# Linear attention with a gated channel mix on one core: q (batches 3 to 7) and y (batches 6 and 7) transposed by DMA in place of TensorE

## The chip, the cores and the metric

The kernel runs on one core of one Trainium2 chip. The metric is the device time of one execution in microseconds (us), the median of several runs. Matmuls run on TensorE (PE, its weight loads PEld), elementwise work on VectorE (DVE) and ScalarE (ACT). GpSimd (POOL) asks for the loads, SyncE (SP) for the stores.

## The reference

Eight batches, eight heads, 576 tokens, head size 64; then a channel mix of 512 channels with 1024 hidden ones:

```python
kv = np.einsum('bhsd,bhse->bhde', k, v)
out = np.einsum('bhsd,bhde->bhse', q, kv)
rms = np.sqrt(np.mean(out * out, axis=-1, keepdims=True) + 1e-06)
x = heads_side_by_side(out / rms * g_norm)              # B, S, 512
x_prev = x shifted by one token, zero first
xk = mu_k * x + (1.0 - mu_k) * x_prev
xr = mu_r * x + (1.0 - mu_r) * x_prev
k = np.maximum(xk @ w_k, 0.0)
v = k * k @ w_v
r = 1.0 / (1.0 + np.exp(-(xr @ w_r)))
return r * v
```

## The kernel before, in words

One loop runs over the batches, b = 0 to 7. In each, TensorE goes through three stages of units, and `mix` writes out the order of all engines by hand: after unit i of a stage the steps that `put(stage, i, ...)` listed are issued. K is the first product: eight units (`km`), each with eight matmuls into `ps_km`, a relu on ACT into `rt` and a square into `sqk` on DVE or ACT (`ACT_SQ`). R is the gate (`r`): four or five tiles of 128 tokens into `ps_r`, a sigmoid on ACT. V is the second product (`vv`): two half units a tile into `ps_v`, then a product with the sigmoid on DVE (`finish`) and two stores on SP's queue. Even batches have four tiles, odd ones five, as two batches share nine. An engine takes its instructions in the order in which they were issued.

Between these units stands the attention of later batches. While batch b is mixed, a = b+1 gets its last attention steps and a2 = b+2 its first (in batches 2 to 5 fully so):

- `kv`: 72 matmuls on quadrants of TensorE (64x64), two copies to SBUF.
- `qt`: 72 transposes of q on TensorE (L188) into `ps_qt`, copied to `qT` by ACT (three) and DVE (one) (L113, L115).
- `u`: 40 matmuls qT by kv into `ps_u` (L210); `square` on ACT and `reduce` on DVE give the sums of squares `ss`.
- `newton`: eight small DVE instructions for 1/rms; `mult` writes y = u/rms on DVE (L253).
- `flip`, `flip0`: 36 transposes of y on TensorE (L268) into `ps_x`; `move` (ACT and DVE, L258, L260) scales by g and writes `xT`, channels by tokens.
- `wrap`, `diff`, and `scale` and `add` (together `blend`): the token shift, giving `xk` and `xr` (L343 to L370). The next batch's K needs xk, its R needs xr.

The attention has five PSUM banks in turn (`ps_at`), the mix three (`ps_mm`). The inputs of a batch have one buffer each (`in_k`, `in_v`, `in_q`), so `load_all(b + 3)`, in the order k, v, q on POOL's queue, waits until kv and qt of batch b+2 have read theirs. `out_sb` has seven buffers, `rt` seven, most others two. Batches 0 and 1 have an order of their own.

Of the kernel before, what the change touches and what calls it, by code (L numbers as in the profile page):

```python
# [24 lines left out]
def kernel(  # L25
# [13 lines left out]
    nc = tc.nc  # L39
# [55 lines left out]

    def load_all(b):
        if b < B:
            for name in "kvq":
                x_in[name, b] = inp.tile([128, NHP, GX], BF16, tag=f"in_{name}", name=f"in_{name}")
                nc.gpsimd.dma_start(out=x_in[name, b], in_=by_token(dram[name], b))  # L100

# [120 lines left out]
    def newton(a):  # L222


        ss = at[a]["ss"]
        ms, y, t, s = (mine(a, key, [128, NRG, NHP], FP32) for key in ("ms", "rs", "nt", "ns"))

        def first():
            DVE.tensor_scalar(out=ms, in0=ss, scalar1=1.0 / HD, scalar2=1e-6, op0=ALU.mult, op1=ALU.add)

        def guess():
            DVE.tensor_scalar(out=y.bitcast(I32), in0=ms.bitcast(I32), scalar1=-0.5,
                              scalar2=float(0x5F1FFFF9), op0=ALU.mult, op1=ALU.add)

        def squared():
            DVE.tensor_mul(out=t, in0=y, in1=y)

        def halve(c):
            DVE.scalar_tensor_tensor(out=s, in0=t, scalar=c, in1=ms, op0=ALU.mult, op1=ALU.mult)

        def update(c):
            DVE.scalar_tensor_tensor(out=y, in0=s, scalar=c, in1=y, op0=ALU.add, op1=ALU.mult)

        steps = [first, guess]
        for c in (0.703952253, 0.5):
            steps += [squared, lambda c=c: halve(-c), lambda c=c: update(1.5 if c == 0.5 else c * 2.38924456)]
        return steps

    def mult(a, t0, n, Ms):
        y, rs, cts = mine(a, "y", [128, NRG, NHP, HD], BF16), at[a]["rs"], span(Ms)  # L250
        for i, ps in enumerate(at[a]["u", t0, n, Ms]):
            g = rg(t0, n, i) if n else slice(0, 1)
            DVE.tensor_mul(out=y[:, g, cts], in0=ps,  # L253
                           in1=rs[:, g, cts].unsqueeze(3).to_broadcast([128, max(n, 1), 2 * len(Ms), HD]))

    def move(eng, dst, src):
        if eng is ACT:
# [115 lines left out]
    def km_part(b, fcs, c0, c1, dst, eng=ACT, which=ps_mm):  # L373
        ps = bank(which, [128, len(fcs), c1 - c0], FP32, "ps_km")
        for n, fc in enumerate(fcs):
            for cc in range(NHP):
                nc.tensor.matmul(ps[:, n, :], wk_sb[:, cc, 128 * fc:128 * fc + 128], at[b]["xk"][:, cc, c0:c1],  # L377
                                 start=(cc == 0), stop=(cc == NHP - 1))
# [20 lines left out]

    sig, hold, later = {}, {}, {}  # L400

    def r(t):
        ps = bank(ps_mm, [128, C], FP32, "ps_r")
        for cc in range(NHP):
            nc.tensor.matmul(ps, xr[:, cc, 128 * t:128 * t + 128], wr_sb[:, cc, :],  # L405
                             start=(cc == 0), stop=(cc == NHP - 1))
        sig[t] = work.tile([128, C], BF16, tag="sig", name="sig", bufs=6)
        ACT.activation(out=sig[t], in_=ps, func=AF.Sigmoid)  # L408
# [31 lines left out]
    def mix(b, plan):  # L440
# [15 lines left out]
        units += [("R", i, lambda t=t: r(t)) for i, t in enumerate(tiles)]  # L456
# [75 lines left out]
    rs_c("y1", odd, *lx)  # L532

    every = slice(0, NHP)
    for b in range(B):
        a, a2 = b + 1, b + 2
        plan = {}

        def put(stage, i, *steps):
            plan.setdefault((stage, i), []).extend(steps)  # L540
# [2 lines left out]
            return lambda: f(*args)  # L543

        load_all(b + 3)

        def attend(a, stage, i):

            put(stage, i, on(kv, a, ALL, (ACT, ACT)), on(qt, a, 0, (ACT, DVE)), on(qt, a, 1, (ACT, ACT)))

        def all_u(a, stage, i):
            put(stage, i, on(u, a, 2, 2, ALL), on(u, a, 0, 2, ALL), on(u, a, 0, 0, ALL),
                on(square, a, 2, 2, ALL), on(square, a, 0, 2, ALL), on(square, a, 0, 0, ALL))

        def mults(a):
            return [on(mult, a, 2, 2, ALL), on(mult, a, 0, 2, ALL), on(mult, a, 0, 0, ALL)]

        def flips(a):
            return [on(flip, a, 0, 4, ALL, (ACT, DVE)), on(flip0, a, (ACT, ACT))]

        def blend(a, which, eng=DVE):
# [33 lines left out]
        elif b == 1:  # L595
            br = blend(1, 1)
            put("K", 1, on(kv, a, ALL, (ACT, ACT), (ps_at, ps_at)))
            put("K", 3, on(qt, a, 0, (ACT, DVE)), on(qt, a, 1, (DVE, DVE)))
            put("K", 4, *br[:3])
            put("K", 5, *br[3:])  # L600
            put("K", 6, part_square(1, slice(0, 8), *hi1))
            put("K", 7, on(u, a, 2, 2, ALL), on(u, a, 0, 2, ALL), on(u, a, 0, 0, ALL), on(square, a, 2, 2, ALL),
                on(reduce, a, 5, 9, ALL))
            put("K", 8, on(square, a, 0, 2, ALL), part_square(1, slice(0, 2), *lo1))
            put("K", 9, on(square, a, 0, 0, ALL))
            put("K", 10, part_square(1, slice(2, 4), *lo1), on(reduce, a, 0, 5, ALL))
            put("K", 11, part_square(1, slice(4, 6), *lo1), part_square(1, slice(6, 8), *lo1))
            put("R", 1, lambda a=a: run(newton(a)))
            put("R", 4, mults(a)[0])
            put("V", 0, mults(a)[1], mults(a)[2])  # L610
            put("V", 4, *flips(a))
            put("V", 5, on(wrap, a), on(diff, a, every), on(kv, a2, ALL, (ACT, ACT)))
            put("V", 6, *blend(a, 0), on(qt, a2, 0, (ACT, DVE)), on(qt, a2, 1, (ACT, ACT)))
            all_u(a2, "V", 8)
        elif a < B:
            if b == 2:
                br = blend(2, 1)
                put("K", 0, *br[:3])
                put("K", 1, *br[3:])
                put("K", 2, on(reduce, a, 5, 9, ALL))  # L620
                put("K", 3, on(reduce, a, 0, 5, ALL))
                put("K", 5, lambda a=a: run(newton(a)[:4]))
                put("K", 6, lambda a=a: run(newton(a)[4:]))
                put("K", 7, mults(a)[0])
                put("R", 0, mults(a)[1])
                put("R", 1, mults(a)[2])
                put("V", 0, on(kv, a2, ALL, (ACT, ACT)), on(qt, a2, 0, (ACT, DVE)),
                    on(flip, a, 0, 4, ALL, (ACT, DVE)), on(flip0, a, (DVE, DVE)), on(wrap, a), on(diff, a, every))
                put("V", 1, on(qt, a2, 1, (ACT, ACT)))
                put("V", 2, *blend(a, 0)[:3])  # L630
# [31 lines left out]
_INS = ['q', 'k', 'v', 'g_norm', 'moe_mu_k', 'moe_mu_r', 'moe_w_k', 'moe_w_v', 'moe_w_r']  # L662
# [26 lines left out]
```

## Time and profile before

| | |
|---|---|
| Time, median of 3 runs (lowest to highest) | 207.17 us (206.87 to 207.18) |
| Span of the profiled execution, first to last instruction | 205.0 us |
| Time of the profiled execution around its span | not listed apart; the median is 2.2 us above the span |
| Granted TensorE clock | 1.000 |
| ps_v, ps_km, ps_r on PE | 62.0, 65.1 and 32.1 us busy |
| ps_qt on PE (504 transposes) | 6.3 us busy |
| ps_x on PE (252 transposes) | 5.6 us busy |
| Loads of k, v, q, issue to landing | 7.9, 11.1 and 13.8 us |

A profile is one execution; times are us from the start of the span. L12 is line 12 of the kernel. Busy times count an instruction from start to end, and matmuls overlap, so a sum over a group can exceed the time it holds the engine; the chain of waits gives the time that a group holds alone. "idle <-X" names what ended an engine's idle time. The chain follows back from the last instruction to what released it, or to the instruction before it on the same engine.

### The profile page before, as it was taken

What the parts mean: (1) busy time and instruction counts of PE and PEld (TensorE: products, weight loads), DVE (VectorE), ACT (ScalarE), POOL (GpSimd) and SP (SyncE); (2) the same over time, 40 slices, a digit from 0 to 9 for tenths busy, and PEclk for the clock granted to TensorE, in tenths of its full rate; (3) what the DMA queues carried; (4) which work ended last, traced back from release to release, by engine and by line L of the source; (5) the groups of instructions that cost most, each with busy time, mean ns of one, the idle gap of its engine ahead of it and who ended that gap; (6) DMA issues with size and microseconds to landing.
All of it is one profiled execution on the core that took longest, in us unless ns stands there. A gap on an engine that the chain in (4) does not pass through costs nothing.

```text
span 205.0 us, 6284 instructions
## 1 busy us (share of the span) xinstructions
PE 191.3 (93%) x2654; PEld 115.7 (56%) x2684; DVE 156.6 (76%) x333; ACT 137.7 (67%) x290; POOL 24.9 (12%) x40
## 2 busy tenths in 40 slices
PE   7778989999998899999999999999999999999992
PEld 2335854585444685557554674567554674476451
DVE  2479959989979598889879695999688794984131
ACT  2378784578725789868997389868986489267400
POOL 7940130040004000400021000400000000000000
PEclk9999999999999999999999999999999999999999
DMA  6999999999937990799009960599004600160055
GB/s 219 211 205 207 206 208 199 209 212 179 172 67 125 220 207 0 104 209 240 5 8 170 254 180 0 72 224 258 5 3 107 155 0 3 42 155 9 3 121 135
DMA packets 21360, 27.22 MB, mean 133 GB/s; under 512 B 1740, under 2 KB 16340, under 8 KB 21332
## 3 DMA queue, kind: packets, MB, share of 16 engines
q0 software_dynamic: 14848, 16.19, 48.7%
q1 hardware_dynamic: 6244, 10.36, 18.1%
q8 instruction: 21, 0.34, 0.7%
q10 hardware_dynamic: 240, 0.26, 0.4%
q14 instruction: 7, 0.06, 0.1%
HBM read 33.56 MB, written 9.44 MB: 210 GB/s over the span
## 4 chain that ended last, share of the span: by engine, by line
PE 75%; DVE 10%; ACT 6%; DMA 4%; issue 2%; POOL 1%; DVEq 0%; ACTq 0%; POOLq 0%
PE ps_v L415 27%; PE ps_km L377 26%; PE ps_r L405 12%; DMA rt<-in_v_dram 4%; PE ps_u L210 3%; PE ps_x L268 2%; PE ps_kv L174 2%; PE ps_qt L188 2%; ACT sqk L386 1%; ACT rt L380 1%; DVE ss L220 1%; DVE y L253 1%; DVE m L355 1%; DVE sqk L388 1%; ACT sig L408 1%
## 5 line engine op out<-in xcount | busy, mean ns | idle before, releaser
L380 ACT ACTIVATE rt<-ps_km 128x288 bf16<-128x288 f32 (+3 forms) x120 | 50.9, 429 | 21.6 <-PE ps_km L377 13.8
L377 PE MATMUL ps_km<-xk,wk_sb 128*128 128x288 bf16 (+4 forms) x512 | 65.1, 286 | 0.2
L415 PE MATMUL ps_v<-wv_sb,sqk 128*128 128x512 bf16 x265 | 62.0, 379 | 1.8 <-issue 1.4
L377 PEld LDWEIGHTS <-wk_sb 128*128 128x128 bf16 x512 | 49.3, 98 | 15.4 <-issue 1.0
L415 PEld LDWEIGHTS <-sqk 128*128 128x128 bf16 x280 | 26.1, 98 | 30.0 <-issue 0.2
L432 DVE TENSOR_TENSOR out_sb<-ps_v,sig 128x512 f32<-128x512 f32 (+1 forms) x37 | 24.6, 672 | 15.6 <-PE ps_v L415 14.0
L405 PE MATMUL ps_r<-wr_sb,xr 128*128 128x512 bf16 x132 | 32.1, 379 | 0.6
L408 ACT ACTIVATE sig<-ps_r 128x512 bf16<-128x512 f32 x36 | 21.3, 610 | 2.9 <-PE ps_r L405 2.9
L388 DVE TENSOR_TENSOR sqk<-rt 128x576 bf16<-128x576 bf16 (+4 forms) x39 | 19.0, 506 | 4.7 <-ACT rt L380 4.7
L405 PEld LDWEIGHTS <-xr 128*128 128x128 bf16 x144 | 13.7, 98 | 15.1 <-issue 0.3
L216 ACT ACTIVATE sq<-ps_u 128x512 bf16<-128x512 f32 (+1 forms) x35 | 16.6, 564 | 7.2 <-PE ps_u L210 7.2
L253 DVE TENSOR_TENSOR y<-ps_u,rs 128x512 bf16<-128x512 f32 (+1 forms) x35 | 19.8, 628 | 0.3
L220 DVE TENSOR_REDUCE ss<-sq 128x16 f32<-128x1024 bf16 (+1 forms) x14 | 18.4, 1345 | 1.8 <-ACT sq L216 1.8
L258 ACT ACTIVATE xT<-ps_x,cols 128x128 bf16<-128x128 bf16 (+2 forms) x22 | 12.4, 645 | 8.3 <-PE ps_x L268 8.3
L100 POOL DMA_DIRECT2D in_k<-in_k_dram x7 | 5.2, 746 | 101.5 <-PE ps_kv L174 101.5
L113 ACT COPY qT<-ps_qt 128x576 bf16<-128x576 bf16 x19 | 11.4, 648 | 8.8 <-PE ps_qt L314 6.3
L355 DVE TENSOR_SCALAR m<-dx,cols 128x576 bf16<-128x576 bf16 (+2 forms) x52 | 16.2, 357 | 0.2
L347 DVE TENSOR_TENSOR dx<-xT 128x2304 bf16<-128x2304 bf16 (+4 forms) x11 | 11.3, 1029 | 4.1 <-ACT xT L258 3.8
L386 ACT ACTIVATE sqk<-rt 128x576 bf16<-128x576 bf16 x18 | 12.4, 687 | 0.0
L370 DVE TENSOR_TENSOR xr<-m,xT 128x1152 bf16<-128x1152 bf16 x16 | 11.7, 754 | 0.2
L370 DVE TENSOR_TENSOR xk<-m,xT 128x1152 bf16<-128x1152 bf16 (+2 forms) x16 | 11.2, 704 | 0.5
L353 ACT ACTIVATE m<-dx,cols 128x576 bf16<-128x576 bf16 (+2 forms) x14 | 9.4, 725 | 2.5 <-DVE dx L347 2.5
(64 smaller groups left out, 131.6 us busy)
## 6 DMA issues: line engine op xcount, KB each, us to landing
out_dram<-out_sb SPq DMA_DIRECT2D x69, 128.0 KB, 3.6
in_k<-in_k_dram POOLq DMA_DIRECT2D x7, 576.0 KB, 7.9
in_v<-in_v_dram POOLq DMA_DIRECT2D x7, 576.0 KB, 11.1
in_q<-in_q_dram POOLq DMA_DIRECT2D x7, 576.0 KB, 13.8
wk_sb<-in_moe_w_k_dram POOLq DMA_DIRECT2D x2, 512.0 KB, 9.1
wv_sb<-in_moe_w_v_dram POOLq DMA_DIRECT2D x2, 512.0 KB, 21.5
sqk<-in_k_dram SPq DMA_DIRECT2D x1, 576.0 KB
q<-in_q_dram POOLq DMA_DIRECT2D x2, 288.0 KB, 6.4
```

Of the source, the lines that this page charges most:

```text
L216: ACT.activation(out=sq[:, rg(t0, n, i) if n else slice(0, 1), span(Ms)], in_=ps, func=AF.Square)
L220: DVE.tensor_reduce(out=ss[:, g0:g1, span(Ms)], in_=sq[:, g0:g1, span(Ms)], op=ALU.add, axis=AX.X)
L253: DVE.tensor_mul(out=y[:, g, cts], in0=ps, in1=rs[:, g, cts].unsqueeze(3).to_broadcast([128, max(n, 1), 2 * len(Ms), HD]))
L355: eng.tensor_scalar(out=out_, in0=in_, scalar1=mu, scalar2=None, op0=ALU.mult)
L370: DVE.tensor_add(out=dst, in0=m[:, hs, c0:c1], in1=x[:, hs, c0:c1])
L377: nc.tensor.matmul(ps[:, n, :], wk_sb[:, cc, 128 * fc:128 * fc + 128], at[b]["xk"][:, cc, c0:c1], start=(cc == 0), stop=(cc == NHP - 1))
L380: eng.activation(out=dst, in_=ps, func=AF.Relu)
L388: eng.tensor_mul(out=sqk[:, fcs, o:o + n], in0=src, in1=src)
L405: nc.tensor.matmul(ps, xr[:, cc, 128 * t:128 * t + 128], wr_sb[:, cc, :], start=(cc == 0), stop=(cc == NHP - 1))
L408: ACT.activation(out=sig[t], in_=ps, func=AF.Sigmoid)
L415: nc.tensor.matmul(ps, sqk[:, fc, 128 * t:128 * t + 128], wv_sb[:, fc, :], start=(fc == 0), stop=(fc == NFC - 1))
L432: DVE.tensor_mul(out=o, in0=hold[t], in1=sig[t][:, c])
```

## The change

`qt_d` replaces `qt` for batches 3 to 7: one transposing DMA from SP's queue turns the whole q tile of 128x2304 into 18 blocks of 128x128. In such a block head channels stand on the upper or the lower half of the partitions by the parity of the token group, so `kv_d` writes kv a second time with its halves swapped (four more copies on ACT), and `u_d` and `u0_d` work in 72 matmuls on quadrants. `square_d`, `reduce_d` and `mult_d` are the same steps in the new layout. From batch 4 on, loads are asked for in the order q, k, v.

For batches 6 and 7 `flip_d` turns y by six transposing DMAs a batch straight into `xT`, in place of `flip`, `flip0` and `move`. The scaling by g, which `move` did, goes into copies of two weights, `wkg` and `wrg`, which eight POOL instructions, issued in batch 5, write; K and R of batches 6 and 7 use them. For 3 to 5 `flip_p` is `flip` in the new layout.

The order changes with it. In batches 2 to 4 newton and mult stand at K4 to K7, the flip of y with wrap and diff at V0, the blends at V1 to V3 and the adds for xr at K0 of the next batch; kv stands at V1, the transposing DMA of q at K6 and u at V5. In batches 5 and 6 mult stands at K0 to K2 with flip_d right behind each, newton in the batch before. The cut diff:

```diff
+    wkg = const.tile([128, NHP, F], BF16, name="wkg")
+    wrg = const.tile([128, NHP, C], BF16, name="wrg")
...
-            for name in "kvq":
+            for name in "kvq" if b < 4 else "qkv":
                 x_in[name, b] = inp.tile([128, NHP, GX], BF16, tag=f"in_{name}", name=f"in_{name}")
                 nc.gpsimd.dma_start(out=x_in[name, b], in_=by_token(dram[name], b))
...
+    NJ = G // 2
+    NQ = NHP * S // 128
+
+    def qt_d(a):
+        qT_ = at[a]["qT"] = work.tile([128, NQ, 128], BF16, tag="qT", name="qT")
+        nc.sync.dma_start_transpose(out=qT_, in_=x_in["q", a].rearrange("p m x -> p (m x)"))
+
+    def kv_d(a, engines, shifts):
+
+        dst = at[a]["kv"] = work.tile([128, 2, 2, 2, HD], BF16, tag="kv", name="kv")
+        kb, vb = x_in["k", a], x_in["v", a]
+        ps = [bank(ps_at, [128, 2, HD], FP32, "ps_kv") for _ in range(2)]
+        for M in range(2):
+            for j in range(G):
+                for e in range(2):
+                    for i in range(2):
+                        nc.tensor.matmul(ps[e][half(i), M, :], kb[half(e), 2 * M + i, tok(j)],
+                                         vb[half(e), 2 * M + i, tok(j)], start=(j == 0), stop=(j == G - 1))
+        for e in range(2):
+            evac(engines[e], dst[:, 0, e], ps[e])
+        for e in range(2):
+            for i in range(2):
+                evac(shifts[e], dst[half(1 - i), 1, e], ps[e][half(i)])
+
+    def u_one(a, out_, m, e, j):
+        par = (m + j) % 2
+        nc.tensor.matmul(out_, at[a]["qT"][half(par), (G * m + j) // 2, half(e)],
+                         at[a]["kv"][half(par), int(m % 2 != par), e, m // 2, :], start=True, stop=True)
+
+    def u_d(a, t0):
+
+        ps = at[a]["u", t0] = [bank(ps_at, [128, 2, 2, 2, HD], FP32, "ps_u") for _ in range(2)]
+        for t in range(2):
+            for mh in range(2):
+                for e in range(2):
+                    for mp in range(2):
+                        for r in range(2):
+                            u_one(a, ps[mp][half(r), t, mh, e, :], 2 * mh + mp, e, 2 * (t0 + t) + 1 + r)
+
+    def u0_d(a):
+
+        ps = at[a]["u", None] = [bank(ps_at, [128, 2, 2, HD], FP32, "ps_u")]
+        for mh in range(2):
+            for e in range(2):
+                for mp in range(2):
+                    u_one(a, ps[0][half(mp), mh, e, :], 2 * mh + mp, e, 0)
...
+    def mult_d(a, t0):
+        rs = at[a]["rs"]
+        if "yd" not in at[a]:
+            t_ = work.tile([128, 4 * NRG, HD], BF16, tag="y", name="y")
+            at[a]["yd"] = t_[:, 4:].rearrange("p (t h) d -> p t h d", t=NJ), t_[:, 0:4]
...
+    def flip_p(a, engines):
+        y, y0 = at[a]["yd"]
+        ps = [bank(ps_at, [128, NHP, NJ, P], BF16, "ps_x") for _ in range(2)]
+        for t in range(NJ):
+            for hp in range(NHP):
+                for r in range(2):
+                    nc.tensor.transpose(ps[r][:, hp, t, :], y[half(r), t, 2 * hp:2 * hp + 2].rearrange("p e d -> p (e d)"),
+                                        ident[half(r), half(r)])
+        for r in range(2):
+            move(engines[r], blocks(a)[:, :, 1 + r:8 + r:2, :], ps[r])
...
+    def flip_d(a, t0):
+        y, y0 = at[a]["yd"]
+        if t0 is None:
+            for mp in range(2):
+                nc.sync.dma_start_transpose(out=xT[a % 2][:, mp::2, P:2 * P],
+                                            in_=y0[half(mp)].rearrange("p h d -> p (h d)"))
+        else:
+            for t in range(t0, t0 + 2):
+                c0 = P + P * (2 * t + 1)
+                nc.sync.dma_start_transpose(out=xT[a % 2][:, :, c0:c0 + 2 * P], in_=y[:, t].rearrange("p h d -> p (h d)"))
...
-                nc.tensor.matmul(ps[:, n, :], wk_sb[:, cc, 128 * fc:128 * fc + 128], at[b]["xk"][:, cc, c0:c1],
+                nc.tensor.matmul(ps[:, n, :], (wkg if b >= FROM_Y else wk_sb)[:, cc, 128 * fc:128 * fc + 128], at[b]["xk"][:, cc, c0:c1],
...
-            nc.tensor.matmul(ps, xr[:, cc, 128 * t:128 * t + 128], wr_sb[:, cc, :],
+            nc.tensor.matmul(ps, xr[:, cc, 128 * t:128 * t + 128], (wrg if b >= FROM_Y else wr_sb)[:, cc, :],
...
+    FROM_Q, FROM_Y = 3, 6
...
-
-        def attend(a, stage, i):
-
-            put(stage, i, on(kv, a, ALL, (ACT, ACT)), on(qt, a, 0, (ACT, DVE)), on(qt, a, 1, (ACT, ACT)))
+        if b == FROM_Y - 1:
+            for dst, src in ((wkg, wk_sb), (wrg, wr_sb)):
+                for cc in range(NHP):
+                    POOL.tensor_scalar(out=dst[:, cc], in0=src[:, cc], scalar1=g_sb, scalar2=None, op0=ALU.mult)
...
         def mults(a):
+            if a >= FROM_Q:
+                return [on(mult_d, a, 2), on(mult_d, a, 0), on(mult_d, a, None)]
             return [on(mult, a, 2, 2, ALL), on(mult, a, 0, 2, ALL), on(mult, a, 0, 0, ALL)]
 
+        def turns(a):
+            return [on(flip_d, a, 2), on(flip_d, a, 0), on(flip_d, a, None)]
+
+        def sums(a):
+            if a >= FROM_Q:
+                return [on(reduce_d, a, 20, 36), on(reduce_d, a, 0, 20)]
+            return [on(reduce, a, 5, 9, ALL), on(reduce, a, 0, 5, ALL)]
+
         def flips(a):
+            if a >= FROM_Q:
+                return [on(flip_p, a, (ACT, DVE)), on(flip0_p, a, (ACT, ACT))]
...
-            put("V", 5, on(wrap, a), on(diff, a, every), on(kv, a2, ALL, (ACT, ACT)))
-            put("V", 6, *blend(a, 0), on(qt, a2, 0, (ACT, DVE)), on(qt, a2, 1, (ACT, ACT)))
+            put("V", 0, on(qt_d, a2))
+            put("V", 5, on(wrap, a), on(diff, a, every), on(kv_d, a2, (ACT, ACT), (ACT, ACT)))
+            put("V", 6, *blend(a, 0))
             all_u(a2, "V", 8)
-                put("K", 2, on(reduce, a, 5, 9, ALL))
-                put("K", 3, on(reduce, a, 0, 5, ALL))
-                put("K", 5, lambda a=a: run(newton(a)[:4]))
-                put("K", 6, lambda a=a: run(newton(a)[4:]))
-                put("K", 7, mults(a)[0])
-                put("R", 0, mults(a)[1])
-                put("R", 1, mults(a)[2])
-                put("V", 0, on(kv, a2, ALL, (ACT, ACT)), on(qt, a2, 0, (ACT, DVE)),
-                    on(flip, a, 0, 4, ALL, (ACT, DVE)), on(flip0, a, (DVE, DVE)), on(wrap, a), on(diff, a, every))
-                put("V", 1, on(qt, a2, 1, (ACT, ACT)))
-                put("V", 2, *blend(a, 0)[:3])
-                put("V", 3, *blend(a, 0)[3:])
-                br = 4
+            elif a < FROM_Y:
+                put("K", 0, on(add, b, 1, A), on(add, b, 1, Z))
+            if a < FROM_Y:
+                put("K", 2, *(sums(a) if b == 2 else []))
+                put("K", 4, lambda a=a: run(newton(a)))
+                put("K", 5, mults(a)[0])
+                put("K", 6, mults(a)[1])
+                put("K", 7, mults(a)[2])
+                put("V", 0, *flips(a), on(wrap, a), on(diff, a, every))
             else:
-                put("K", 2, lambda a=a: run(newton(a)[:4]))
-                put("K", 3, lambda a=a: run(newton(a)[4:]))
-                put("K", 4, mults(a)[0])
-                put("K", 5, mults(a)[1])
-                put("K", 6, mults(a)[2])
-                put("R", 2, *flips(a))
-                put("R", 3, on(wrap, a), on(diff, a, every))
-                put("V", 0, *blend(a, 0)[:3])
-                put("V", 1, *blend(a, 0)[3:])
-                br = 2
-            bl = blend(a, 1, ACT)
-            put("V", br, *(bl[:2] if b > 2 else []), *bl[3:5])
-            if 2 < b < B - 2:
-                put("V", br + 1, bl[2])
-                put("V", br + 2, bl[5])
+                if b < B - 2:
+                    put("K", 0, on(qt_d, a2))
+                put("K", 0, mults(a)[0], turns(a)[0])
+                put("K", 1, on(add, b, 1, A), on(add, b, 1, Z), mults(a)[1], turns(a)[1])
+                put("K", 2, mults(a)[2], turns(a)[2])
+                put("V", int(b < B - 2), on(wrap, a), on(diff, a, every))
+            bk, bl = blend(a, 0, ACT if b == B - 2 else DVE), blend(a, 1, ACT)
+            put("V", 1, *bk[:3])
+            put("V", 2, *bk[3:])
+            put("V", 3, *bl[:2], *bl[3:5])
+        else:
+            put("K", 0, on(add, b, 1, A), on(add, b, 1, Z))
...
-        if b in (3, B - 1):
-            put("K", 0, *([on(scale, b, 1, 0), on(scale, b, 1, 1)] if b == 3 else []), on(add, b, 1, A))
-            put("K", 1, on(add, b, 1, Z))
         if b > 1 and a2 < B:
-            if b > 2:
-                attend(a2, "V", 0)
-            all_u(a2, "V", 4 + int(b == 2))
-            put("V", nV - 1, on(reduce, a2, 5, 9, ALL), on(reduce, a2, 0, 5, ALL))
+            if a < FROM_Y:
+                put("K", 6, on(qt_d, a2))
+            put("V", 1, on(kv_d, a2, (ACT, ACT), (ACT, ACT)))
+            all_u(a2, "V", 5 if a < FROM_Y else 3)
+            put("V", nV - 1, *sums(a2))
+            if a2 >= FROM_Y:
+                put("V", nV - 1, lambda: run(newton(a2)))
```

More of the change, by code (lines that the diff above doesn't have):

```diff
@@ L225, in newton @@
         ss = at[a]["ss"]
-        ms, y, t, s = (mine(a, key, [128, NRG, NHP], FP32) for key in ("ms", "rs", "nt", "ns"))
+        ms, y, t, s = (mine(a, key, ss.shape, FP32) for key in ("ms", "rs", "nt", "ns"))
         def first():
@@ new lines, in u0_d, with square_d @@
+    def u0_d(a):
[4 more added lines that the diff above has]
+                    u_one(a, ps[0][half(mp), mh, e, :], 2 * mh + mp, e, 0)
+    def square_d(a, t0):
+        sq = mine(a, "sq", [128, 4 * NRG, HD], BF16)
+        for mp, ps in enumerate(at[a]["u", t0]):
+            if t0 is None:
+                ACT.activation(out=sq[:, 0:4], in_=ps.rearrange("p m e d -> p (m e) d"), func=AF.Square)
+            else:
+                out_ = sq[:, 4:].rearrange("p (t c h) d -> p t c (h d)", t=NJ, c=2)[:, t0:t0 + 2, mp]
+                ACT.activation(out=out_, in_=ps.rearrange("p t m e d -> p t (m e d)"), func=AF.Square)
@@ new lines, in reduce_d @@
+    def reduce_d(a, lo, hi):
+        sq, ss = at[a]["sq"], mine(a, "ss", [128, 4 * NRG], FP32)
+        DVE.tensor_reduce(out=ss[:, lo:hi], in_=sq[:, lo:hi], op=ALU.add, axis=AX.X)
+    def mult_d(a, t0):
[4 more added lines that the diff above has]
+        y, y0 = at[a]["yd"]
+        for mp, ps in enumerate(at[a]["u", t0]):
+            if t0 is None:
+                DVE.tensor_mul(out=y0, in0=ps.rearrange("p m e d -> p (m e) d"),
+                               in1=rs[:, 0:4].unsqueeze(2).to_broadcast([128, 4, HD]))
+            else:
+                out_ = y[:, t0:t0 + 2].rearrange("p t (m c e) d -> p c t m e d", c=2, e=2)[:, mp]
+                rs_ = rs[:, 4:].rearrange("p (t c m e) -> p c t m e", t=NJ, c=2, m=2)[:, mp, t0:t0 + 2]
+                DVE.tensor_mul(out=out_, in0=ps, in1=rs_.unsqueeze(4).to_broadcast([128, 2, 2, 2, HD]))
@@ new lines, in flip0_p @@
+    def flip0_p(a, engines):
+        y, y0 = at[a]["yd"]
+        ps = [bank(ps_at, [128, 2, P], BF16, "ps_x0") for _ in range(2)]
+        for mh in range(2):
+            for mp in range(2):
+                nc.tensor.transpose(ps[mp][:, mh, :], y0[half(mp), 2 * mh:2 * mh + 2].rearrange("p e d -> p (e d)"),
+                                    ident[half(mp), half(mp)])
+        for mp in range(2):
+            move(engines[mp], blocks(a)[:, mp::2, 0, :], ps[mp])
+    def flip_d(a, t0):
+        y, y0 = at[a]["yd"]
+        if t0 is None:
+            for mp in range(2):
+                nc.sync.dma_start_transpose(out=xT[a % 2][:, mp::2, P:2 * P],
+                                            in_=y0[half(mp)].rearrange("p h d -> p (h d)"))
+        else:
+            for t in range(t0, t0 + 2):
+                c0 = P + P * (2 * t + 1)
+                nc.sync.dma_start_transpose(out=xT[a % 2][:, :, c0:c0 + 2 * P], in_=y[:, t].rearrange("p h d -> p (h d)"))
@@ L400, with r @@
     sig, hold, later = {}, {}, {}
-    def r(t):
+    def r(b, t):
         ps = bank(ps_mm, [128, C], FP32, "ps_r")
         for cc in range(NHP):
-            nc.tensor.matmul(ps, xr[:, cc, 128 * t:128 * t + 128], wr_sb[:, cc, :],
+            nc.tensor.matmul(ps, xr[:, cc, 128 * t:128 * t + 128], (wrg if b >= FROM_Y else wr_sb)[:, cc, :],
                              start=(cc == 0), stop=(cc == NHP - 1))
@@ L455, in mix @@
             units = [("K", i, lambda i=i: km(b, i)) for i in range(NFC)]
-        units += [("R", i, lambda t=t: r(t)) for i, t in enumerate(tiles)]
+        units += [("R", i, lambda t=t: r(b, t)) for i, t in enumerate(tiles)]
         order = [(t, part) for t in tiles for part in range(2)]
@@ L545 @@
         load_all(b + 3)
-        def attend(a, stage, i):
-            put(stage, i, on(kv, a, ALL, (ACT, ACT)), on(qt, a, 0, (ACT, DVE)), on(qt, a, 1, (ACT, ACT)))
+        if b == FROM_Y - 1:
+            for dst, src in ((wkg, wk_sb), (wrg, wr_sb)):
+                for cc in range(NHP):
+                    POOL.tensor_scalar(out=dst[:, cc], in0=src[:, cc], scalar1=g_sb, scalar2=None, op0=ALU.mult)
         def all_u(a, stage, i):
+            if a >= FROM_Q:
+                put(stage, i, on(u_d, a, 2), on(u_d, a, 0), on(u0_d, a),
+                    on(square_d, a, 2), on(square_d, a, 0), on(square_d, a, None))
+                return
             put(stage, i, on(u, a, 2, 2, ALL), on(u, a, 0, 2, ALL), on(u, a, 0, 0, ALL),
@@ L555, in mults @@
         def mults(a):
+            if a >= FROM_Q:
+                return [on(mult_d, a, 2), on(mult_d, a, 0), on(mult_d, a, None)]
             return [on(mult, a, 2, 2, ALL), on(mult, a, 0, 2, ALL), on(mult, a, 0, 0, ALL)]
+        def turns(a):
[4 more added lines that the diff above has]
+            return [on(reduce, a, 5, 9, ALL), on(reduce, a, 0, 5, ALL)]
         def flips(a):
+            if a >= FROM_Q:
+                return [on(flip_p, a, (ACT, DVE)), on(flip0_p, a, (ACT, ACT))]
             return [on(flip, a, 0, 4, ALL, (ACT, DVE)), on(flip0, a, (ACT, ACT))]
@@ L649 @@
+            bk, bl = blend(a, 0, ACT if b == B - 2 else DVE), blend(a, 1, ACT)
+            put("V", 1, *bk[:3])
+            put("V", 2, *bk[3:])
+            put("V", 3, *bl[:2], *bl[3:5])
+        else:
+            put("K", 0, on(add, b, 1, A), on(add, b, 1, Z))
         if 1 < b < B - 1:
```

## The prediction

> **What bounds the kernel now.** I read the busy times first, then the chain of waits by line, then the timeline of one whole batch, and last the batches whose chain leaves PE. The page opens with
>
> ```profile
> PE 191.3 (93%) x2654; PEld 115.7 (56%) x2684; DVE 156.6 (76%) x333; ACT 137.7 (67%) x290; POOL 24.9 (12%) x40
> PE 75%; DVE 10%; ACT 6%; DMA 4%; issue 2%; POOL 1%; DVEq 0%; ACTq 0%; POOLq 0%
> ```
>
> PE is busy 93% of the span and carries 75% of the chain. In batch 4 the chain (start us, us, what) is all PE, so there a matmul taken out is time taken out:
>
> ```profile
> 115.34 7.84 PE ps_km L377 x64
> ...
> 125.77 0.63 PE ps_x L268 x36
> ...
> 128.23 0.71 PE ps_kv L174 x72
> 128.94 0.70 PE ps_qt L188 x72
> 129.64 0.16 issue
> 129.80 3.45 PE ps_v L415 x15
> 133.25 0.82 PE ps_u L210 x40
> 134.06 0.16 issue
> ```
>
> K starts (first ps_km in the timeline, batches 2 to 7) at 68.91, 90.72, 115.17, 136.59, 160.56 and 179.74, so the batches take 21.81, 24.45, 21.42, 23.97 and 19.18 us. Batches 4 and 5 are dense; 3 is 0.48 longer than 5, its equal in work. Below, K+x is x us after a batch's K start; V0 is its first half tile of ps_v. Work sums are K 7.84, one R tile (four 512-column matmuls) 0.865, one V tile 1.73.
>
> **What goes from PE.** (1) The 72 transposes of q for batches 5, 6 and 7 lie dense in batches 3 to 5: 3 x 0.70 = 2.10. (2) Those for batch 4 are split in batch 2: halves of about 0.35 and 0.41, a further 0.16 issue, and 0.20 in which ps_x waits for ACT's qT copy: 1.1. (3) Those for batch 3 lie in batch 1 and hold more:
>
> ```profile
> 64.29 0.29 PE L188 MATMUL ps_qt<-ident,in_q 64*64 64x64 bf16 x12 [0.55 <-issue]
> 66.07 0.76 DVE L370 TENSOR_TENSOR xk<-m,xT 128x1152 bf16<-128x1152 bf16 x1
> 67.25 0.85 PE L210 MATMUL ps_u<-kv,qT 64*128 64x64 bf16 x38 [0.71 <-DVE qT L115]
> ```
>
> The visit lasts from 63.06 to 64.73 (1.67) and ps_u waits 0.71: 2.4. But K of batch 2 needs xk, whose last add ends at 66.83 by a DVE chain that stays; K can move from 68.91 to about 66.9: 2.0. (4) u becomes 72 quadrant matmuls; kv has 72 of that form in 0.71 against u's 0.82: 5 x 0.11 = 0.55. (5) The transposes of y for 6 and 7: 2 x 0.63 = 1.26. (6) y's transposes move from R2 to V0 in batch 3, where they now wait for the mults; the 0.48 goes. Gross: 2.10 + 1.1 + 2.0 + 0.55 + 1.26 + 0.48 = 7.5.
>
> **What is late next.** I walked each engine's order with the durations of the trace. DVE loses the qT copy (0.45) but gets the flip's move, wrap, diff and blend in V, where its queue was already tight. These are its rows in batch 4:
>
> ```profile
> 115.98 2.60 DVE L220 TENSOR_REDUCE ss<-sq 128x16 f32<-128x1024 bf16 x2
> 121.91 2.81 DVE L253 TENSOR_TENSOR y<-ps_u,rs 128x512 bf16<-128x512 f32 x5
> 126.41 0.75 DVE L260 TENSOR_SCALAR xT<-ps_x,cols 128x1024 bf16<-128x1024 bf16 x1 [1.69 <-PE ps_x L268]
> 128.35 1.36 DVE L347 TENSOR_TENSOR dx<-xT 128x2304 bf16<-128x2304 bf16 x1 [0.93 <-ACT xT L258]
> 129.75 0.66 DVE L355 TENSOR_SCALAR m<-dx,cols 128x576 bf16<-128x576 bf16 x2
> 130.44 0.76 DVE L370 TENSOR_TENSOR xk<-m,xT 128x1152 bf16<-128x1152 bf16 x1
> ```
>
> Batch 4 after: V0 ends at K+12.2 (7.84 + 4 x 0.865 + 0.865), flips at 12.8, ACT's three moves (1.65) at 14.5, diff at 15.9, the output product of tile 0 (0.65) at 16.5, two blends (0.66 + 0.69 each) at 19.2. PE goes on with V1, kv, three tiles and u and reaches the next K at 20.8. So xk has 1.6 us of cover; without it each us of DVE delay is a us of PE. The products of the last tiles come at 21 to 22, so the ring of three ps_mm banks costs K about 0.2. In front of V0 the mults end near 11.5 against 12.2, covered. For batch 2 DVE has two more blends (2.7) in K: the mults end at 12.8 as before (81.73) against 12.2, 0.6 of wait, and the banks then cost batch 3 0.5. In 5 and 6 the mults of y come ahead of the xr adds in K: last product 0.9, reduce to 3.3, newton 5.1, square and first mult 6.7, square and adds 8.5, while R wants xr at 7.9 to 8.3: 0.4 each. Sum: 0.2 + 0.6 + 0.5 + 0.8 = 2.1.
>
> ACT loses three qT copies (1.72) a batch and gains four shifts of kv (pairs of such copies take 0.44, so 0.9): less work, and u is four units behind kv. Held loads: q of b+3 is asked for after the transposing DMA at K6, k and v after kv at V1. POOL asked for k, v, q at 129.29 to 130.75 and they land 7.9, 11.1 and 13.8 later; all are wanted a batch (20 us) on. Zero, as long as the transpose lands before V; POOL has nothing but loads behind it there.
>
> **Transposing DMAs: no row shows one.** The nearest by size:
>
> ```profile
> out_dram<-out_sb SPq DMA_DIRECT2D x69, 128.0 KB, 3.6
> in_k<-in_k_dram POOLq DMA_DIRECT2D x7, 576.0 KB, 7.9
> ```
> q, 576 KB: by the load, 7.9. Asked for at K6 (K+6.9) and wanted at V5 (K+18), there are 11 us; in batch 1, from 56.2 (q landed: DMA share falls to 0.05 by 57) to u at about 64.5, 8.3. Free by this row; at five times it, about 25 us too late in every batch. I take 0, the row being the nearest in size. On SP the stores queue behind it: the next come in V, and out_sb has seven buffers.
>
> y, six DMAs a batch (four of 128 KB, two of 32 KB): mults at K+6.7, 9.8, 10.3, the last DMAs asked for at about 10.4, SP waiting on nothing else. wrap and diff open a DVE chain to xk that is 4.4 us long; the next K is wanted at 22.6 in batch 5 and 18.4 in batch 6, and the banks want the products in between, so y must have landed by 16.3 and 14.3. With stores' 3.6 from issue, overlapped as stores are, the last lands at 14.0: 0. One after the other at 3.6, they land at 6.7 + 6 x 3.6 = 28.3: 12 + 14 = 26 us. I take 0.5, near the first, since stores do overlap.
>
> **The copies with g** are eight POOL multiplies (four 128x1024, four 128x512), behind the loads of batch 7, so from about K+16.2 of batch 4; needed a batch later. POOL's rows have no such one. Its memset of 128 columns takes 0.229 against 0.104 for one, its affine select 0.290: 1.0 to 1.4 ns a column, 6.9 to 9.7 us for all. POOL has 20. Below: 0. Above, if DVE must wait for each: next section. Beside POOL's loads at 129.29 to 131.5 DVE's add took 0.76 and its scales 0.33 each, as elsewhere; nearest to that I take 1.0 (two DVE instructions that meet one of 1.3 each, less 1.6 cover).
>
> **Sum.** 7.5 gained, 2.1 + 0.5 + 1.0 lost: 3.9 off the span of 205.0, giving 201.1. The runs' median of 207.17 is 2.2 above the span (launch and end, not touched): 203.3.
>
> **Rivals.** (A) *POOL's copies stop DVE*, slower. Six DVE instructions (four scales, two adds, all on SBUF alone) stand before xk of batch 5 when POOL starts. If each loses one POOL instruction (four of 1.1 to 1.6, two of 0.6 to 0.85), xk is 5.4 to 7.7 late, less 1.6 cover: K of batch 5 stands 3.8 to 6.1. DVE then owes the products behind it, and banks and xr hold PE 2 to 3.4 more: 5.8 to 9.5, say 7 in place of my 1.0: 209.3. It decides from 4.9 us of lock. Against it: no slower DVE row beside POOL's loads; for it: these read and write SBUF over whole rows, which no row of POOL does here. The Trainium skill (SBUF — State Buffer, "Who interferes with whom") has the rule: GpSimd shares a port pair with VectorE, held for a whole instruction, and a VectorE instruction with two SBUF inputs, or a scalar multiply in a fast mode, blocks. By that rule the time is this rival's; the trace has no GpSimd arithmetic beside VectorE and can't show it.
>
> (B) *The transposing DMAs are slow or go one by one.* Serial y gives 26 us, 229; half so, 216. It is slower than before once y lands some 2.2 us late in each of both batches (past K+18.5 and 16.5), or q past u by 0.8 in each of five. For it: nothing here transposes by DMA, small pieces; against: DMA engines stand almost idle in these K stages (GB/s 5 and 3 from 143 to 154, 0 and 3 from 164 to 174).
>
> (C) *DVE takes the bound*: it is busy 16 to 17 of 20 us already. If the walk's covers (0.7 before V0, 1.6 before xk) fail by 1 us in four batches and a DVE wait lasts into the next, 2.5 is lost: 205.8, still faster. For: 76% mean, serial chain; against: a batch's DVE work sums to about 20 of 20.8.
>
> (D) *All new terms hidden* (POOL, y and half the new waits): 203.3 - 1.0 - 0.5 - 1.0 = 200.8.
>
> (E) *The DMAs only replace PE work that was hidden*: excluded for batches 3 to 6, where the chain is PE throughout; part of batch 1's 2.0 could be so, in C.
>
> **How the numbers follow.** Forecast 0.40, A 0.22, B 0.12, C 0.14, D 0.12. Within 0.2% (0.4 us), what a measurement of this kernel tells from none, lies only a strip between C and A: 0.05. Faster: forecast, D, most of C and some of A where the lock is partial: 0.64. Slower: the rest of A, and B: 0.31. Range: from D's 200.5 to A's upper side, 209.7; outside lie B and A's worst. The forecast's own range, over my bounds on POOL (0 to 3) and y (0 to 1.5), is 201.8 to 206.3.
>
> **What would show it.** Right: no ps_qt after batch 1, no ps_x in 5 and 6, ps_v right behind kv; batches 4 and 5 near 20.8 and 23.0; PE busy near 185. Lateness of DVE: ps_km or ps_x idle <- DVE. A: DVE's scales and adds longer than 0.33 and 0.76 beside POOL's multiplies, K of batch 5 waiting for xk. B: dx waiting for a DMA in 5 and 6, ps_u for qT. Wrong altogether if K of batch 2 doesn't move to about 67.

## The result: 3.3% slower, and the profile after

The changed kernel takes 213.84 us (213.55 to 214.75, four runs) against 207.14 before: a ratio of 1.0334, 95% interval 1.0312 to 1.0356. The forecast was 203.3 us; the direction was wrong, and 213.84 lies outside the range. The profiled execution spans 212.0 us. The busy times and the chain by engine, on the page after:

```profile
PE 192.7 (91%) x2412; PEld 112.4 (53%) x2412; DVE 160.9 (76%) x322; ACT 133.9 (63%) x293; POOL 43.4 (20%) x48
PE 61%; DVE 16%; ACT 8%; DMA 7%; issue 4%; SPq 1%; POOL 1%; DVEq 0%; ACTq 0%; POOLq 0%
```

The trace has 242 fewer matmuls on PE, but its part of the chain fell from 75% to 61% and DVE's rose from 10% to 16%. Up to K of batch 4 things go much as forecast: K of batches 2, 3 and 4 starts at 66.93, 88.40 and 111.87 in place of 68.91, 90.72 and 115.17, so 3.3 us are gained by then. After that the starts of batches 5 to 7 are 137.38, 164.73 and 186.46, where they were 136.59, 160.56 and 179.74. The chain from batch 4 to 5 (start us, us, what):

```profile
112.03 7.84 PE ps_km L486 x64
...
124.80 1.63 ACT xT L367 x3
126.46 0.06 DVE dx L456
126.52 1.21 issue
127.73 0.68 DVE out_sb L541
128.41 2.29 DVE m L464 x2
130.72 1.55 DVE xk L479
132.27 2.89 DVE m L464 x2
135.18 0.06 DVE xk L479
...
137.33 2.27 DVE m L464 x2
139.60 0.60 DVE out_sb L541
...
140.25 9.58 PE ps_km L486 x60
```

A pair of scales (`m`), 0.66 before, takes 2.3 to 2.9 here, and an add (`xk`), 0.76 before, 1.55. At the same time POOL is at the copies with g, and PE waits for a bank behind DVE's products (timeline):

```profile
128.57 12.13 POOL L659 TENSOR_SCALAR wkg<-wk_sb,cols 128x1024 bf16<-128x1024 bf16 x4
...
137.38 0.86 PE L486 MATMUL ps_km<-xk,wk_sb 128*128 128x288 bf16 x4 [4.47 <-DVE out_sb L541]
...
140.69 6.23 POOL L659 TENSOR_SCALAR wrg<-wr_sb,cols 128x512 bf16<-128x512 bf16 x4
```

The copies last 18 us, not 7 to 10. A further thing shows in the windows of the same profile (after the times: busy us of PE, PEld, DVE, ACT, POOL; then PE's granted clock, DMA share, GB/s):

```profile
134.00:136.00 2.00, 0.00 (x0) 0.00 (x0) 1.97 (x2) 0.00 (x0) 2.00 (x2) 1.00 1.19 223
138.00:140.00 2.00, 0.24 (x2) 0.00 (x0) 2.00 (x3) 0.41 (x1) 2.00 (x1) 0.50 0.58 131
142.00:144.00 2.00, 2.00 (x10) 1.20 (x9) 1.97 (x2) 0.82 (x2) 2.00 (x3) 0.50 0.80 182
```

After 4.5 us in which PE stands idle its granted clock is half until about 144.5, so ten matmuls of K go into 2 us, where eighteen do at 1.00 (e5, below).

In batch 6 the loss comes from the other unknown, the transposing DMAs of y (timeline: SP's queue, then the DVE instruction that waits, `diff`, and PE behind it):

```profile
171.66 5.36 SPq L363 DMA_TRANSPOSE xT<-y  x4
...
177.13 3.35 SPq L358 DMA_TRANSPOSE xT<-y  x2
181.83 1.36 DVE L456 TENSOR_TENSOR dx<-xT 128x2304 bf16<-128x2304 bf16 x1 [5.76 <-DMA xT<-y]
...
183.84 1.89 PE L524 MATMUL ps_v<-wv_sb,sqk 128*128 128x512 bf16 x8 [2.11 <-DVE out_sb L541]
```

SP holds each of them 1.2 us or more, the small ones as long as the large. The diff opens 6.6 us after the last product of y has ended (175.20), and it and the products behind it on DVE come too late for PE. The DMA issues of the page (median us to landing) show no slow transfer, as far as landings are recorded; for y that is four of the twelve, all of 128 KB:

```profile
xT<-y SPq DMA_TRANSPOSE x12, 2.4
qT<-in_q SPq DMA_TRANSPOSE x5, 6.4
```

### The profile page after: what moved, and what is told of

Read it like the earlier page. It is cut to its first block, busy times and chain, and to the rows that moved or that the text cites. A ratio compares the mean times of both kernels' runs of the same rounds, so it can differ in the third digit from the quotient of the medians.

```text
span 212.0 us, 5806 instructions
## 1 busy us (share of the span) xinstructions
PE 192.7 (91%) x2412; PEld 112.4 (53%) x2412; DVE 160.9 (76%) x322; ACT 133.9 (63%) x293; POOL 43.4 (20%) x48
## 4 chain that ended last, share of the span: by engine, by line
PE 61%; DVE 16%; ACT 8%; DMA 7%; issue 4%; SPq 1%; POOL 1%; DVEq 0%; ACTq 0%; POOLq 0%
PE ps_km L486 25%; PE ps_v L524 18%; PE ps_r L514 12%; DVE m L464 5%; DVE out_sb L541 4%; DMA rt<-in_v_dram 3%; DMA out_dram<-out_sb 2%; ACT sig L517 2%; DVE xk L479 2%; ACT sqk L495 2%; ACT xT L367 1%; ACT rt L489 1%; DVE ss L316 1%; PE ps_kv L274 1%; PE ps_u L284 1%
## 5 line engine op out<-in xcount | busy, mean ns | idle before, releaser
L486 PE MATMUL ps_km<-xk,wk_sb 128*128 128x288 bf16 (+4 forms) x384 | 51.6, 294 | 6.7 <-DVE out_sb L541 6.5
L486 PEld LDWEIGHTS <-wk_sb 128*128 128x128 bf16 x384 | 37.7, 100 | 20.1 <-issue 7.9
L541 DVE TENSOR_TENSOR out_sb<-ps_v,sig 128x512 f32<-128x512 f32 (+1 forms) x37 | 24.4, 670 | 14.3 <-PE ps_v L524 8.1
L514 PE MATMUL ps_r<-wr_sb,xr 128*128 128x512 bf16 x108 | 24.3, 379 | 0.0
L464 DVE TENSOR_SCALAR m<-dx,cols 128x576 bf16<-128x576 bf16 (+2 forms) x50 | 21.2, 470 | 0.1
L102 POOL DMA_DIRECT2D in_q<-in_q_dram x7 | 5.3, 754 | 68.6 <-DMA qT<-in_q 66.8
L486 PE MATMUL ps_km<-xk,wkg 128*128 128x288 bf16 x128 | 16.3, 286 | 1.2 <-DVE out_sb L541 1.2
L486 PEld LDWEIGHTS <-wkg 128*128 128x128 bf16 x128 | 12.5, 98 | 5.3 <-issue 1.7
L312 ACT ACTIVATE sq<-ps_u 128x512 bf16<-128x512 f32 x20 | 10.3, 602 | 4.6 <-PE ps_u L284 4.6
L316 DVE TENSOR_REDUCE ss<-sq 128x16 f32<-128x1024 bf16 (+1 forms) x10 | 13.0, 1341 | 0.0
L331 DVE TENSOR_TENSOR y<-ps_u,rs 128x512 bf16<-128x512 f32 x20 | 12.6, 681 | 0.1
```

Of the source, the lines that this page charges most:

```text
L316: DVE.tensor_reduce(out=ss[:, lo:hi], in_=sq[:, lo:hi], op=ALU.add, axis=AX.X)
L331: DVE.tensor_mul(out=out_, in0=ps, in1=rs_.unsqueeze(4).to_broadcast([128, 2, 2, 2, HD]))
L464: eng.tensor_scalar(out=out_, in0=in_, scalar1=mu, scalar2=None, op0=ALU.mult)
L486: nc.tensor.matmul(ps[:, n, :], (wkg if b >= FROM_Y else wk_sb)[:, cc, 128 * fc:128 * fc + 128], at[b]["xk"][:, cc, c0:c1], start=(cc == 0 ...
L514: nc.tensor.matmul(ps, xr[:, cc, 128 * t:128 * t + 128], (wrg if b >= FROM_Y else wr_sb)[:, cc, :], start=(cc == 0), stop=(cc == NHP - 1))
L541: DVE.tensor_mul(out=o, in0=hold[t], in1=sig[t][:, c])
```

## The experiments

Each is compared with the kernel before in the same session; "+" is slower. "Only q" is the change without the DMAs of y and without copies (`FROM_Y = 8`).

**Which part costs what.** First the copies on DVE, then q alone, then POOL's work with nothing that reads its results, in the new kernel and in the old.

```diff
 e1: -  POOL.tensor_scalar(out=dst[:, cc], in0=src[:, cc], scalar1=g_sb, ...)      # issued first in batch 5
     +  DVE.tensor_scalar(out=dst[:, cc], in0=src[:, cc], scalar1=g_sb, ...)       # the eight, put("R", 3) in batch 5
 e2: -  FROM_Q, FROM_Y = 3, 6      +  FROM_Q, FROM_Y = 3, 8      and no copies
 e3: e2 and POOL's eight multiplies as in the change
 e4: the kernel before and POOL's eight multiplies
```

> The changed kernel, with the eight multiplies by g on DVE at the end of R in batch 5 (where DVE stands idle for 3.5 us) in place of POOL. Theory L (POOL's multiplies stretch DVE's scales from 0.37 to 1.3 us and adds from 0.76 to 1.55, and the wait of PE that follows halves its clock): the 5.0 us of batch 4 and 4.7 us of batch 5 above their dense length go, batch 6's wait for y stays: 204.4 us (203.5 to 205.5). Theory O (the new order of DVE in V holds K of batch 5, whatever POOL does): no change, 212 to 214 us.

> Only q by transposing DMA (batches 3 to 7); y of all batches by TensorE, no weight copies, no POOL multiplies. Theory L: batches 1 to 3 keep the 3.3 us that the changed kernel is ahead at K of batch 4, batches 4 and 5 add 0.7 to 1 each: 202.4 us (201.5 to 203.5). Theory O: K of batch 5 is late here as well, 208 to 212 us.

> Only q by transposing DMA, with the eight POOL multiplies issued as in the change; nothing reads their results. Theory L: they cost some 9 us here too, 211 us (208 to 214). Theory Y (the loss is in the six transposing DMAs of y and what waits for them): as without them, 202.4 us.

> The kernel before, with the eight POOL multiplies behind the loads of batch 7; nothing reads their results. Theory L: the cost goes with POOL and DVE and not with the DMAs; DVE has one scale pair, one add and a pair for xr left in V when POOL starts, so it is somewhat less than in the changed kernel: 212 us (210 to 215). Theory Y or O: 207.1 us, no change.

Measured: e1 206.17 us (ratio 0.9979, 0.9959 to 1.0000; -0.6), e2 203.19 (0.9817, 0.9797 to 0.9837; -3.6), e3 211.81 (1.0237, 1.0205 to 1.0268; +5.0), e4 214.10 (1.0346, 1.0312 to 1.0380; +7.3). Theory L holds: POOL's multiplies cost 8.6 us with q only, 7.3 in the kernel before, and 7.3 in the change (+6.7 against -0.6). In e2 batch 4 is dense, as it was walked (first matmuls of K, batches 4 and 5):

```profile
111.50 8.00 PE L486 MATMUL ps_km<-xk,wk_sb 128*128 128x288 bf16 x64
132.38 8.00 PE L486 MATMUL ps_km<-xk,wk_sb 128*128 128x288 bf16 x64
```

In e1 the same eight copies are small on DVE, in its idle stretch before V of batch 5 (groups of DVE, 140 to 148 us; busy us, mean ns):

```profile
L759 DVE TENSOR_SCALAR wkg<-wk_sb,cols 128x1024 bf16<-128x1024 bf16 x4 | 1.7, 481 | 0.0
L759 DVE TENSOR_SCALAR wrg<-wr_sb,cols 128x512 bf16<-128x512 bf16 x4 | 1.1, 349 | 0.0
```

So the parts are: q -3.6, y by DMA with its copies on DVE +3.0 (e1 against e2, which differ in the order of batches 5 and 6 too), POOL in place of DVE +7.3. They are differences of neighbouring runs, so that they sum to +6.7 proves nothing more. e1 was forecast at 204.4 (203.5 to 205.5) and missed by 1.8: its batch 5 takes 24.1 us, where theory L left 22.7 (27.4 less 4.7), so y's DMAs cost something there as well. In e4 the estimate of 5 was low too. How y stands in e1, without POOL (SP's two small issues, diff, and PE behind it; K of batch 6 starts at 156.78):

```profile
169.54 2.71 SPq L358 DMA_TRANSPOSE xT<-y  x2
173.60 1.36 DVE L456 TENSOR_TENSOR dx<-xT 128x2304 bf16<-128x2304 bf16 x1 [5.12 <-DMA xT<-y]
175.61 1.89 PE L524 MATMUL ps_v<-wv_sb,sqk 128*128 128x512 bf16 x8 [1.46 <-DVE out_sb L541]
```

**The clock, and how POOL stops DVE.**

```diff
 e5: the change, and at the end of V in batch 4
     +  for _ in range(40): nc.tensor.matmul(unused half of u's bank, zeros[:, :128], zeros[:, :256], ...)
 e6: e3 with each multiply in pieces of 128 columns (48 instructions)
 e7: e3 with  POOL.memset(dst[:, cc], 0.0)  three times over, in place of the multiplies
 e12: e2, and in batch 7 four POOL multiplies of 128x1024 that wait for the last square
```

> The changed kernel with 40 matmuls of zeros (256 columns, some 4.3 us) on PE at the end of batch 4, in the gap before K of batch 5; their result, in the unused half of a u bank, is not read. Theory C (the granted clock of 0.5 from 138 to 144 us follows from PE's 4.5 us of idleness and is a cost of its own): the clock stays at 1, K of batch 5 loses the 2.2 us that it takes longer (9.6 in place of 7.4 for its last 60 matmuls): 211.5 us (211 to 212.5). Theory D (K of batch 5 is paced by DVE, which hands back banks and squares, and the clock only follows): 213.8 us, no change.

> Only q by transposing DMA, with POOL's multiplies (results not read) cut into 48 of 128 columns each. Theory H (the port is held for a whole POOL instruction and the other waits): a DVE instruction waits for at most one piece of about 0.4 us, so DVE loses some 3 us in place of 9 and PE 1 to 2: 204 to 206 us. Theory S (while POOL reads and writes, DVE's instructions run at a lower rate, however POOL's work is cut): as with eight multiplies, 211 to 213 us.

> Only q by transposing DMA, with 24 POOL memsets (1024 or 512 columns, three rounds over the copies' tiles, some 18 us by 1 ns a column; nothing reads them) in place of the multiplies: POOL writes and reads nothing. Theory R (DVE's adds, with two inputs in SBUF, lose to POOL's reads alone; its scales also to writes): scales stretched, adds 0.76; DVE loses about half, 204 to 207 us. Theory W (any POOL instruction on SBUF): scales and adds both stretched, 210 us and more. Theory N (only reads count): 203.2 us.

> Only q by transposing DMA, and in batch 7 four POOL multiplies of 128x1024 (source sqk, results not read) that wait for the last square, at a time when DVE has only products with one SBUF input. If a multiply takes 1.1 to 1.6 us there, its 3.0 us in the change came from waiting for DVE; if 3.0, that is POOL's own rate, and DVE alone waited. Time near 203 us in either case.

e5: 212.34 us (1.0266, 1.0245 to 1.0288; +5.5 against +6.7). The clock stays at 1.00 and the last 60 matmuls of K take 7.62 us in place of 9.58:

```profile
142.00:144.00 2.00, 2.00 (x18) 1.60 (x17) 1.93 (x3) 1.68 (x5) 2.00 (x3) 1.00 0.87 196
```

So the half clock follows from the idleness and is a cost of its own, some 2 us in K. Little of it reaches the end, since R then waits 1.6 us for xr from the still late DVE: each theory had a part of it. The time falls by 1.2 us, but the two profiles put only 0.6 of that into batches 4 and 5 together (52.9 and 52.3 us); batch 6, where no zeros stand, is 0.9 shorter too (21.7 and 20.8), as y's last DMAs are issued without the 2.07 us that one of them took in the change. What the clock alone costs in the end is therefore known only as about 0.6 to 1.2 us.

e12: 203.39 us, one run. DVE is idle until 190.41 and then has only products with one SBUF input; POOL still takes 2.8 us for each multiply:

```profile
185.31 11.32 POOL L765 TENSOR_SCALAR wkg<-sqk,cols 128x1024 bf16<-128x1024 bf16 x4 [56.71 <-DVE sqk L497]
```

This is POOL's own rate (3.0 in the change), so DVE, not POOL, did most of the waiting.

e6: 203.15 us (0.9817, 0.9800 to 0.9833; -3.7). In pieces the same work costs nothing measurable (q only: 203.19), though POOL takes 34 us for it (DVE and POOL by time):

```profile
129.44 0.86 DVE L464 TENSOR_SCALAR m<-dx,cols 128x576 bf16<-128x576 bf16 x2
129.68 22.57 POOL L661 TENSOR_SCALAR wkg<-wk_sb,cols 128x128 bf16<-128x128 bf16 x32
130.33 0.81 DVE L479 TENSOR_TENSOR xk<-m,xT 128x1152 bf16<-128x1152 bf16 x1
```

Theory S (a lower rate however the work is cut) falls. H is the nearer one, but 203.15 lies below its 204 to 206: a scale takes 0.38 to 0.47 us and an add 0.80 here, so DVE hardly waits. POOL does: a piece takes 0.594 us at the least and up to 1.8.

e7: 217.93 us (1.0536, 1.0520 to 1.0552; +11.1), far above what theory R allowed. The timeline tells why:

```profile
131.89 0.76 DVE L479 TENSOR_TENSOR xk<-m,xT 128x1152 bf16<-128x1152 bf16 x1
132.56 0.68 DVE L541 TENSOR_TENSOR out_sb<-ps_v,sig 128x512 f32<-128x512 f32 x1
133.16 12.78 DVE L464 TENSOR_SCALAR m<-dx,cols 128x576 bf16<-128x576 bf16 x2
```

The memsets end at 145.5, and the first scale of the pair, which alone took 12.50 us, with them. Two adds, which have two inputs in SBUF, took 0.76 beside memsets, 1.55 beside the multiplies. So R's distinction is right (writes stop the scales, not the adds), W (210 us and more) has the time but not the adds, and R's time is wrong. Short memsets in a row left this scale no gap, where POOL's pieces with reads did. It is not so each time: the two pairs before it took 1.41 and 1.42 us beside the same memsets, and these runs don't show what was different for the third. The Trainium skill (SBUF — State Buffer, "Who interferes with whom") says that a VectorE instruction with two SBUF inputs contends with GpSimd's reads and not with an instruction that only writes, and a fast scalar multiply with either; the 0.76, the 1.55 and the 12.78 agree. It also says that the one that comes second blocks until the other's instruction ends. e6 is in keeping with that; the scales of 0.6 to 1.8 us beside multiplies of 3.0 do not show a wait of a whole instruction each time, and to whom the port goes next between POOL's instructions these runs don't settle.

**y by DMA.**

```diff
 e8:  e1, with token group 0 of y by four transposes on PE and two ACT copies at R3, not two DMAs
 e11: e8, with batch 7's y on PE and the plain weights in batch 7
 e13: e8, with groups 1 to 4 on PE as well: two DMAs a batch, behind the first product of y
```

> The changed kernel with the copies on DVE, and token group 0 of y (the two small transposing DMAs, 1.2 to 2.1 us each on SP's queue) by four transposes on PE and two copies on ACT in R3. Theory I (issue on SP, one after the other, sets when y lands in batch 6): landing 2.5 us or more earlier, batch 6 shorter by about 2: 204.2 us against 206.2 (203.7 to 204.9). Theory T (transfer or completion of the large ones sets it): 206 us, as with all six.

> q by transposing DMA; y so for batch 6 alone and without its token group 0, copies with g on DVE; y of batch 7 on PE. From the runs so far batch 5 takes 23.1 with y by DMA against 23.5, batch 6 takes 19.2 with y on PE against 19.7: theory I gives 203.2 - 0.4 = 202.8 us (202.4 to 203.2). Rival: as with q only, 203.2.

> The changed kernel with the copies with g on DVE, and of y only token groups 5 to 8 (the first product of each batch) by two transposing DMAs; groups 0 to 4 by 20 transposes on PE and copies on ACT and DVE in R3. Theory I (the one after the other issue on SP, begun late by the second product, sets when y is whole): the two DMAs land by K+12, diff opens at about K+13.4 in place of K+15.1, batch 6 is 0.7 to 1.2 shorter than with four, less 0.3 of PE in each batch: 202.7 us (202.3 to 203.1). Rival (the transposing DMAs land late for another reason, however few they are): 203.5 us or more.

e8: 203.21 us (0.9827, 0.9812 to 0.9841; -3.6): two DMAs of 32 KB fewer a batch give 3.0 us, more than theory I had. e13: 202.09 us (0.9771, 0.9754 to 0.9788; -4.7), somewhat below its range too; a version that beats both kernels, and q only by 1.1. SP's issue and DVE's diff of batch 6, first in e8, then in e13:

```profile
162.60 5.36 SPq L373 DMA_TRANSPOSE xT<-y  x4
...
170.76 1.36 DVE L466 TENSOR_TENSOR dx<-xT 128x2304 bf16<-128x2304 bf16 x1 [3.76 <-issue]
```

```profile
163.22 2.50 SPq L381 DMA_TRANSPOSE xT<-y  x2
...
169.59 1.36 DVE L474 TENSOR_TENSOR dx<-xT 128x2304 bf16<-128x2304 bf16 x1 [0.47 <-ACT xT L370]
```

With K of batch 6 at 155.68 and 156.31, diff opens at K+15.1 and K+13.3, in e13 released by ACT's copy. Batch 6 falls from 21.45 (e1) to 19.72 and 19.04 us. So theory I holds in the main: issue one after the other, begun late, sets the landing. The last issue begins at K+14.0 in e1 and K+11.0 in e8, 3.0 earlier, while diff opens only 1.7 earlier. In e8 it stands 4.05 us behind that issue (2.8 in e1; the landings on record take 2.4 to 2.5), and data still trickle at 5 to 10 GB/s until 170.1; the profile names no DMA there but "issue". A slow end of the last transfer, theory T's, thus seems to have a part in e8, which no run settles. e11: 202.68 us (0.9795, 0.9780 to 0.9809; -4.3), as forecast; here the gate of the last 64 tokens of batch 6 lacks g, since their tile is made in batch 7 with the plain weights, so it is no version to use.

**The order and the loads.**

```diff
 e9:  the new order of steps with qt, kv, u, flip as before (no DMA transposes), loads k, v, q
 e10: e2 with  for name in "kvq"  for all batches
```

> Only the new order of steps (mults at K5 to K7, flip, wrap and diff at V0, blends at V1 to V3, xr adds at the next K0, u at V5); q and y transposed on PE as before, loads as before. Theory P (the gain of q only is the 0.7 to 2 us of PE per batch that q's transposes held): about the time before, 206.8 (206.0 to 207.5). Theory O2 (the new order gives a good part of the 3.6 us by itself): 205.5 or less.

> Only q by transposing DMA, with the loads of all batches in the old order k, v, q. q is then asked for at V1 behind k and v and lands near K+6 to K+8 of the next batch, where the transposing DMA is asked for; u follows at K+18. Theory M (there is slack, the hold of the loads matters little): 203.2 us as with q first (202.8 to 203.8). Theory H2 (q late makes u late): 204.5 us or more.

e9: 207.51 us (1.0032, 1.0020 to 1.0043; +0.5). The order gives nothing by itself, it costs 0.5; theory O2 falls. The gain of q is then what PE no longer does, which the chain of e9 in batch 4 still has:

```profile
129.41 0.71 PE ps_kv L176 x72
130.12 0.70 PE ps_qt L190 x72
```

e10: 203.42 us (0.9832, 0.9812 to 0.9851; -3.6), as e2: whether q is asked for first or last changes nothing that can be measured.

## Why the prediction was wrong

**The gain from q was right in kind, and 1.3 us too large.** The sum without y and POOL was 7.5 - 1.26 gained, 1.3 lost (0.2 + 0.6 + 0.5): 4.9 us; e2 has 3.6. Its profile is 4.7 ahead at K of batch 7 and loses 0.7 behind that, where PE waits 0.5 for DVE's products; e9 has the same wait, so it comes with the new order and not with the DMAs. K of batch 2 was to move to 66.9 and stands at 66.93. The DVE covers held: batch 4 takes 20.88 in e2, where 20.8 was walked. q's transposing DMAs (6.4 us to landing, up to 9.7) were in time, in batch 1 by 0.5 us alone (landed at 64.76, u at 65.23). Of rival C only that 0.5 shows in e2.

**The step that failed is the term of POOL's copies, "nearest to that I take 1.0".** It measures 7.3 to 8.6 us. Two things were wrong in it. Its row, POOL's loads beside DVE, is no row for arithmetic on SBUF: it is near in place and not in kind. And its rate, 1.0 to 1.4 ns a column from memset and affine select, is 2.8 to 3.0 for a multiply. Rival A had the mechanism, the place (K of batch 5) and "say 7": xk is whole at K+24.9 in the change and K+19.2 in e2, 5.6 us later, where A had 5.4 to 7.7. It was given 0.22. Where a bound runs from 0 to 9.5 and a mechanism stands behind the upper end, it should have had the greater chance. Neither A nor the sum had the half clock.

**The term of y, "I take 0.5", was the second.** Instead of 1.26 gained less 0.5, and 0.8 for xr, y costs 3.0 (e1 against e2). The walk had y landed at K+14.0 in batch 6 for a limit of 14.3; diff, which waits for it, opens at K+16.8 in e1 and K+17.1 in the change. The page's stores gave time to landing, but what counted most was how long SP holds each issue: six times 1.2 to 2.1 us. So B's "one after the other" was right, at the pace of the issues and not at the 3.6 us of a store, and the truth lay between 0 and 26, near the low end.

The chance of 0.64 for faster thus rested on two small terms, 1.0 and 0.5, without a row of their kind. With A's 7 in place of 1.0 and 3 more for y the sum would have been 212.

**Slips that change nothing.** A's lock adds up to 5.6 to 8.1, not 5.4 to 7.7. A's upper side by its own 9.5 is 211.8, so the range should not have ended at 209.7; 213.84 is beyond either. D gives 200.8, not 200.5, and q at five times the load's 7.9 would be 28 us late, not 25.

## What to carry to other kernels

Work put on an idle engine is priced by what it shares with the busy one: eight POOL multiplies cost 7 to 9 us through DVE; on DVE itself they took 2.8 us of an idle stretch, and cut in small pieces on POOL they cost nothing measurable. A transposing DMA relieved PE where the next step stood some 7 us or more behind its issue, as with q; where the next step waits for it, count the issues on the queue, one after the other, and send few and early ones. When a term has no row of its kind, its upper end belongs in the forecast's own range, not in a rival alone.

## What was not expected of the hardware

- PE stood idle from 132.9 to 137.4 us in the trace of after; its granted clock fell to 0.50 at about 137.7, and was back at 1.00 from 145 on. With zeros multiplied in the gap it stayed at 1.00 (e5).
- A DVE scale of 0.37 us can stand through a whole run of POOL memsets: one took 12.50 us, though two pairs before it got through in 1.4 (e7).
- A POOL multiply by a column of scalars took 2.8 us for 1024 columns with DVE quiet (e12), a memset of the same tile 0.99 (e7), the same multiply on DVE 0.48 (e1).
- SP held a transposing DMA of 32 KB as long as one of 128 KB, mostly 1.2 us; the landings on record, all of 128 KB, took 2.4 to 2.5 us from issue.
